# Random-feature attention with a mixture of experts: one burst of projections for each pair of the last batch, and its attention steps at fixed places

## The chip, the core and the metric

The kernel runs on one core of one Trainium2 chip. The metric is the device time of one execution in microseconds; the kernel before has a median of 872.78 us over three runs. The engines are named as the profile names them: PE (TensorE, with PEld for its weight loads), DVE (VectorE), ACT (ScalarE), POOL (GpSimd), and SP (SyncE), which here only issues DMA transfers.

## What is computed

Two layers, the second fed by the first. The attention has 4 batches, 8 heads, 576 positions, head size 64 and 128 random features:

```python
def phi(x):
    proj = np.einsum('bhsd,md->bhsm', x, omega)
    h = proj - np.sum(x * x, axis=-1, keepdims=True) / 2.0
    h = h - np.max(h, axis=-1, keepdims=True)
    return np.exp(h) / np.sqrt(m)
q_p, k_p = phi(q_s), phi(k_s)
kv = np.einsum('bhsm,bhsd->bhmd', k_p, v)
num = np.einsum('bhsm,bhmd->bhsd', q_p, kv)
den = np.einsum('bhsm,bhm->bhs', q_p, k_p.sum(axis=2))[..., None] + 1e-06
attn = num / den
```

The result, 2304 rows of 512, goes through 4 experts with F = 1024: `out += p[:, e] * (relu(x @ w1[e]) @ w2[e])`.

## The kernel before, in words

**Visits.** The expert part is cut into visits. A visit takes one half (512 of the 1024 hidden columns) of one expert's weights and one block of rows; products in fp32 are made of three matmuls on a high and a low part of each operand (`hh`/`hl`, `w2h`/`w2l` and so on). Four groups of visits follow each other: the first block of rows (functions `first_visit` and `plain`), then eight visits `N0` to `N0 + 7` on the second block of 768 rows (`fast`), then eight on the last rows (`deep`). The change touches the eight `fast` visits, which run from about 280 to 549 us of the trace. The rows of the last block are the output of the attention on the last batch, so the attention of that batch (four pairs of heads, class `Halves`) has to be worked in between the expert matmuls of the `fast` visits.

**A fast visit.** First come 14 small products (L967, 6 matmuls of 384 columns each), called p1 to p7 for each of two column groups. p1, p6, p7 and p4 of a group add onto the same PSUM bank `u`, so PE starts p6 only once ACT has copied p1 out of the bank into an SBUF tile `sum` (L973, `keep`), and p7 only once it has copied p6. Between them `split_w2` makes `w2h` on ACT (L642) and `w2l` on POOL out of freshly loaded `w2r`. Then come six output tiles of 12 matmuls of 512 columns (L830 to L832); of tiles 0, 1 and 2 the first six matmuls are made already among the products. Each finished tile is added to `acc` by DVE (`gather`, L842; in the first of the eight visits ACT does it, L840). Between the tiles the weights of the next visit are prepared (`sides`: four additions on DVE, L761 to L764, then `w1sh` on ACT, L642, and a subtraction on POOL).

**Attention of a pair.** Loads of k, q and v; `square` (POOL) and `lengths` (DVE, L340); projection of keys or queries onto the features (`project`, 16 matmuls, L351, and `project_tails`, 4 matmuls, L366, all on 64 rows of the array); maxima over features (DVE, L371 and L376) and `bias` (L381, L382, result `nbk` or `nbq`); exponentials (ACT, L388 in two halves of four, L395 for the tails, results `kp` and `qp`); `sum_keys` (PE, ACT, DVE), `turn` (transposes of the query features), `numerators`, `invert` (reciprocals, L303) and `times`.

**What sets the order.** The kernel is scheduled by hand: an instruction stands in its engine's queue where the Python code calls it, each engine works its queue in order, and waits on other engines are added. `fast` is a generator; each `yield` is a share, counted 0 (before tile 0's second half) to 6 (after tile 5). The loop at the end of `emit` takes one share after another and, whenever the count of shares is due, one tick of the attention generator (`opening` for the first pair's loads, then `later_ticks`, 12 ticks per pair). PSUM has eight banks that are handed out in rotation (`bank`, eight buffers of one tag). SP's loads carry eight semaphores in turn (`DMAHW0` to `DMAHW7` below): a load waits until the one eight places earlier in SP's queue has landed.

Of the kernel before, what the change touches and what calls it, by code (L numbers as in the profile page):

```python
# [5 lines left out]

F32 = mybir.dt.float32
F32R = mybir.dt.float32r
# [6 lines left out]
def attention_moe(ctx, tc, kT, qT, kd, qd, kn, qn, vn, omT, probs, w1, w2, out):  # L15
# [11 lines left out]
    _, NP, D, _ = kT.shape  # L27
# [3 lines left out]
    E, FP, P, _ = w1.shape  # L31
# [36 lines left out]
    def bank(name):  # L68
        return psum.tile([P, 512], F32, tag="ps", name=name)
# [33 lines left out]
    NV = len(HALVES)  # L103
# [339 lines left out]
    def opening(p, both=False):  # L443

        p.load("k")
        yield
        p.load("q")
        yield
        p.load_v()
        p.load_tails()  # L450
        yield
        p.square("k")
        yield
        p.square("q")
        yield
        p.lengths("k")
        if both:
            p.lengths("q")
        yield
# [71 lines left out]
        p.times(1)  # L531
        yield

    def later_ticks(pairs):

        for p, then in zip(pairs, pairs[1:] + [None]):
            p.project("k")
            p.project_tails("k")
            p.maxima("k")
            p.maxima_tails("k")  # L540
            p.bias("k")
            yield
            p.exp_tails("k")
            p.exp("k", 0)
            p.lengths("q")
            yield
            p.exp("k", 1)
            yield
            p.project("q")
            p.project_tails("q")  # L550
            p.maxima("q")
            p.maxima_tails("q")
            p.bias("q")
            yield
            p.exp_tails("q")
            p.exp("q", 0)
            if then:
                then.load("k")
            yield
            p.exp("q", 1)  # L560
            if then:
                then.load("q")
            yield
            p.sum_keys()
            if then:
                then.load_v()
                then.square("k")
            yield
            p.turn(0)
            yield  # L570
            p.turn(1)
            if then:
                then.square("q")
            yield
            p.numerators(0)
            if then:
                then.lengths("k")
            yield
            p.invert(0)
            p.times(0)  # L580
            p.numerators(1)
            yield
            p.invert(1)
            p.times(1)
            yield

    def visit(u, n, c0, m):
        return (u, *HALVES[n], c0, m)
# [1 line left out]
    BIG = {1: (START, 6 * P), 2: (START + 6 * P, 8 * P)}  # L590
# [5 lines left out]
    N0 = len(visits)  # L596
    visits += [visit(u, n, *BIG[u]) for u in (1, 2) for n in range(NV)]
    DEEP = range(N0 + NV, len(visits))
# [344 lines left out]
    def on_sides2(v):  # L943
        if v in sides2:
            next(sides2[v][1])

    def fast(v):
# [109 lines left out]
        for t in range(tiles):  # L1057
            if t in g2:
                outputs(v, hs, g2[t], t, range(2, FH))
            else:  # L1060
                g2[t] = bank("g2")
                outputs(v, hs, g2[t], t, range(FH))
            gather(v, g2[t], t)
            gathered(v, t)
            if t < 2:
                on_sides2(v + 1)
            next(ready, None)
            for _ in range(2 if t < 4 else 1):
                next(more, None)
            yield 1  # L1070
        for _ in more:
            pass

# [381 lines left out]
    def first_visit(g1):  # L1455
        hs = [relu(ps, 2 * P) for ps in g1[:2]]
        yield 0.5
        for ps in g1[2:]:
            split_w(lo=nc.vector)
            hs.append(relu(ps, 2 * P))  # L1460
            yield 0.5
        split_w(lo=nc.vector)
        split_w(lo=nc.vector)
        yield 0.5
        for t in range(2):
            ps = bank("g2")
            outputs(0, hs, ps, t, range(FH))
            gather(0, ps, t)
            gathered(0, t)
            split_w()  # L1470
            split_w(lo=nc.vector)
            yield 1
# [56 lines left out]
        pairs[3].settle()  # L1529
        yield  # L1530

    def chain(*many):
        for x in many:
            yield from x

    building = build(1)

    def emit():
        pairs, g1 = begin()
        later = [Halves(b, hp) for b in range(1, B) for hp in range(NP)]  # L1540
        windows = {
            0: (first_rest(pairs, opening(later[0], both=True)), 20 / 11),
            3: (joint_ticks(later[:-NP]), 76 / 45.4),
            N0: (chain(opening(later[-NP]), later_ticks(later[-NP:])), 54 / (NV * (BIG[1][1] // P + 1) * 0.8)),
        }
        ticks, n, done, per = iter(()), 0, 0.0, 0
        for v in range(len(visits)):
            if v in windows:
                for _ in ticks:
                    pass  # L1550
                ticks, per = windows[v]
                n, done = 0, 0.0
            for share in first_visit(g1) if v == 0 else deep(v) if v in DEEP else fast(v) if v >= N0 else plain(v):
                done += share
                while n < done * per:
                    next(ticks, None)
                    n += 1
        store(0)
# [62 lines left out]
```

## Time and profile before

| | |
|---|---|
| median of three runs | 872.78 us (871.76 to 873.16) |
| profiled execution | 872.62 us, span 870.8 us |
| PE busy | 865.4 us, 99% of the span |
| DVE, ACT, POOL busy | 578.8, 480.2, 559.6 us |
| DMA moved | 136.04 MB, mean 156 GB/s |
| granted TensorE clock | 1.000 |

The span is the time from the first to the last instruction in the profiled execution; its execution time lies 1.8 us above it. PE is busy nearly without a break, so a change of the time is either work that PE no longer has or a gap that opens or closes in its row. The other engines matter where PE has to wait for them.

### The profile page before, as it was taken

To read this page: it belongs to the slowest core of one execution; us is meant where nothing else is said; L and a number is where in the kernel's file an instruction comes from. 1 tells how busy PE (TensorE), PEld (TensorE's weight loads), DVE (VectorE), ACT (ScalarE), POOL (GpSimd) and SP (SyncE) were. 2 spreads that over 40 slices of the span, in tenths; PEclk is the share of its full clock that TensorE was granted. 3 is DMA by queue.
4 is the path that set the end of the run, shared out by engine and by line. 5 is a ranking of instruction groups with operands and counts; after the bars stand their busy time and mean duration, and the time that the engine had idled before them with its cause. 6 is when DMAs were issued, how large, how long until landed. Compare 5 with 4: busy or idle time off the path is not lost.

```text
span 870.8 us, 13397 instructions
## 1 busy us (share of the span) xinstructions
PE 865.4 (99%) x4791; PEld 752.9 (86%) x4791; DVE 578.8 (66%) x953; ACT 480.2 (55%) x1078; POOL 559.6 (64%) x523
## 2 busy tenths in 40 slices
PE   9999999999999999999999999999999999999998
PEld 9988898989888988989989899888888888888886
DVE  5666566666667547465756657885857577585757
ACT  6786677776774555556545554544534434453442
POOL 6759475655644554354444446769888797988865
PEclk9999999999999999999999999999999999999999
DMA  8765634524521756546274354835352462535222
GB/s 185 193 205 161 214 100 164 177 81 131 184 65 58 284 158 254 195 163 218 75 281 157 135 218 154 269 132 183 85 181 80 139 193 85 158 86 181 70 99 97
DMA packets 67651, 136.04 MB, mean 156 GB/s; under 512 B 10400, under 2 KB 23168, under 8 KB 67584
## 3 DMA queue, kind: packets, MB, share of 16 engines
q1 hardware_dynamic: 57488, 105.24, 36.7%
q0 software_dynamic: 9216, 29.36, 10.3%
q10 hardware_dynamic: 880, 0.57, 0.3%
q8 instruction: 38, 0.62, 0.3%
q14 instruction: 29, 0.24, 0.1%
HBM read 101.06 MB, written 34.10 MB: 155 GB/s over the span
## 4 chain that ended last, share of the span: by engine, by line
PE 95%; DMA 2%; POOL 1%; ACT 0%; SPq 0%; issue 0%; ACTq 0%; DVE 0%; POOLq 0%
PE g L1146 18%; PE g L1115 18%; PE g L967 14%; PE g L830 8%; PE g L831 8%; PE g L832 8%; PE g L815 3%; PE g L816 3%; PE g L817 3%; PE kv L406 2%; PE k_ps L351 2%; PE q_ps L351 1%; PE qt_ps L417 1%; DMA q<-in_qT 1%; PE nd L290 1%; PE nd L289 1%
## 5 line engine op out<-in xcount | busy, mean ns | idle before, releaser
L645 POOL TENSOR_TENSOR w2l<-w2r,w2h 128x512 fp32r<-128x512 f32 x61 | 79.3, 1311 | 76.4 <-ACT w2h L642 65.9
L645 POOL TENSOR_TENSOR w1sl<-w1r,w1sh 128x512 fp32r<-128x512 f32 (+1 forms) x43 | 75.2, 1751 | 59.0 <-ACT w1sh L642 52.7
L830 PE MATMUL g<-w2h,hh 128*128 128x512 f32 x280 | 111.6, 399 | 0.0
L832 PE MATMUL g<-w2h,hl 128*128 128x512 f32 x280 | 109.6, 391 | 0.0
L831 PE MATMUL g<-w2l,hh 128*128 128x512 f32 x280 | 109.5, 391 | 0.0
L645 POOL TENSOR_TENSOR w1al<-w1r,w1ah 128x512 fp32r<-128x512 f32 (+1 forms) x45 | 49.4, 1113 | 60.7 <-ACT w1ah L642 55.4
L1160 DVE TENSOR_TENSOR acc<-g,acc 128x512 f32<-128x512 f32 (+1 forms) x106 | 68.5, 681 | 27.2 <-PE g L1146 27.1
L842 DVE SCALAR_TENSOR_TENSOR acc<-g,pr,acc 128x512 f32<-128x512 f32 x70 | 51.0, 735 | 28.0 <-PE g L832 27.9
L832 PEld LDWEIGHTS g<-w2h,hl 128*128 128x128 f32 x280 | 52.5, 188 | 11.5
L830 PEld LDWEIGHTS g<-w2h,hh 128*128 128x128 f32 x280 | 52.6, 188 | 10.1
L831 PEld LDWEIGHTS g<-w2l,hh 128*128 128x128 f32 x280 | 52.6, 188 | 9.0
L1121 ACT ACTIVATE sum<-g 128x512 f32<-128x512 f32 x48 | 28.8, 600 | 48.1 <-PE g L1115 47.5
L981 ACT ACTIVATE hh<-sum 128x384 fp32r<-128x384 f32 x48 | 25.1, 525 | 50.8 <-DVE sum L979 50.4
L645 POOL TENSOR_TENSOR t_hl<-va,t_hl 128x1024 fp32r<-128x1024 f32 x16 | 38.8, 2426 | 21.2 <-ACT t_hl L642 21.2
L985 DVE SCALAR_TENSOR_TENSOR hl<-sum,hh 128x384 fp32r<-128x384 f32 x48 | 27.4, 575 | 36.9 <-ACT hh L981 36.2
L303 DVE RECIPROCAL dn<-dn 128x256 f32<-128x256 f32 (+1 forms) x24 | 46.5, 1943 | 6.3 <-ACT dn L297 6.2
L645 POOL TENSOR_TENSOR w2s<-w2f,w2s 128x512 fp32r<-128x512 f32 x30 | 38.5, 1308 | 18.1 <-ACT w2s L642 18.1
L1115 PE MATMUL g<-xbh,w1sh 128*128 128x512 f32 x128 | 49.9, 390 | 0.0
L1115 PE MATMUL g<-xbl,w1sh 128*128 128x512 f32 x128 | 49.8, 389 | 0.0
L1115 PE MATMUL g<-xbh,w1sl 128*128 128x512 f32 x128 | 49.8, 389 | 0.0
L979 DVE TENSOR_TENSOR sum<-g,sum 128x384 f32<-128x384 f32 x48 | 26.5, 555 | 33.3 <-PE g L967 27.6
L642 ACT ACTIVATE w1sh<-w1r 128x512 fp32r<-128x512 f32 (+1 forms) x43 | 34.1, 795 | 25.2 <-DVE w1r L764 12.9
(254 smaller groups left out, 2700.4 us busy)
## 6 DMA issues: line engine op xcount, KB each, us to landing
w1r<-in_w SPq DMA_DIRECT2D x54, 512.0 KB, 3.6
w2r<-in_w SPq DMA_DIRECT2D x76, 256.0 KB, 3.0
kept<-w1sh SPq DMA_DIRECT2D x16, 512.0 KB, 5.0
kept<-w1sl SPq DMA_DIRECT2D x16, 512.0 KB, 5.5
w1sh<-kept POOLq DMA_DIRECT2D x16, 512.0 KB, 4.6
w1sl<-kept POOLq DMA_DIRECT2D x16, 512.0 KB, 5.4
kept<-w1ah SPq DMA_DIRECT2D x16, 384.0 KB, 4.8
kept<-w1al SPq DMA_DIRECT2D x16, 384.0 KB, 4.9
```

The costliest lines, as they stand in the source:

```text
L303: nc.vector.reciprocal(dn, dn)
L642: hi.activation(a, t, AF.Copy)
L645: lo.tensor_tensor(c, t, f32(a), ALU.subtract)
L830: nc.tensor.matmul(ps, ha[:, ts_], wa, start=(c == 0), stop=False)
L831: nc.tensor.matmul(ps, ha[:, ts_], wc, start=False, stop=False)
L832: nc.tensor.matmul(ps, hc[:, ts_], wa, start=False, stop=(c == FH - 1))
L842: nc.vector.scalar_tensor_tensor(acc[i], ps, sc, acc[i], ALU.mult, ALU.add)
L967: nc.tensor.matmul(ps, a[:, w], x[:, k], start=(start and k + at == 0), stop=(k == 1 and at == 2), skip_group_check=not start)
L1115: nc.tensor.matmul(ps, a[:, w], x[:, k], start=(start and k + at == 0), stop=(k == 1 and at == 2), skip_group_check=not start)
L1121: nc.scalar.activation(t, P_[g][where], AF.Copy)
L1146: nc.tensor.matmul(ps[:, cs], y[:, w], x[:, cs], start=(start and f + k == 0), stop=(f + k == 3), skip_group_check=not start)
L1160: nc.vector.tensor_tensor(t[:, cs], ps[i][:, cs], t[:, cs], ALU.add)
```

## The change

The generator `later_ticks` (printed above) with its 12 ticks for each of the last four pairs is replaced by a table of steps, `later_steps`. A step is bound to a visit and a share; a pair has nine consecutive steps, which begin at places 2, 15, 24 and 36, counted in shares of the eight visits (seven in each): visit `N0` share 2, `N0 + 2` share 1, `N0 + 3` share 3 and `N0 + 5` share 1.

- Keys and queries of a pair are projected in one burst. The tails of the queries go into free columns of the two banks that hold the tails of the keys (`beside="k"`), so a burst takes six banks. The maxima of the queries are taken only after the exponentials of the keys' tails.
- The loads of the first pair (k, q, v: seven transfers) are issued near the end of visit `N0 - 1`; its squares and lengths come in the first two shares of `N0`. Before, they were ticks inside `N0`.
- The order of a pair's later steps is drawn together: `sum_keys` and the first `turn` stand in one step.
- In `fast`, `yield 1` moves ahead of the preparation of the next visit's weights, so that an attention step bound to a share now stands in front of that preparation on ACT, DVE and POOL.

The number of matmuls does not change.

```diff
-    def later_ticks(pairs):
...
+    def later_steps(pairs, at):
+
+        PER = BIG[1][1] // P + 1
+
+        steps = {}
+
+        def add(v, t, *calls):
+            steps.setdefault((N0 + v + t // PER, t % PER) if v >= 0 <= t else (N0 + v, t), []).extend(calls)
+
+        p = pairs[0]
+        add(-1, 13, partial(p.load, "k"), partial(p.load, "q"), p.load_v, p.load_tails)
+        add(0, 0, partial(p.square, "k"), partial(p.square, "q"))
+        add(0, 1, partial(p.lengths, "k"), partial(p.lengths, "q"))
+
+        for p, then, first in zip(pairs, pairs[1:] + [None], at):
+
+            def projections(p=p):
+                p.project("k")
+                p.project_tails("k")
+                p.project("q")
+                p.project_tails("q", beside="k")
+                largest(p, "k")
+
+            def largest(p, which):
+                p.maxima(which)
+                p.maxima_tails(which)
+                p.bias(which)
+
+            def keys(p=p):
+                p.exp("k", 0)
+                p.exp_tails("k")
+                largest(p, "q")
+
+            def queries(p=p):
+                p.exp("k", 1)
+                p.exp_tails("q")
+                p.exp("q", 0)
...
+            row = [
+                [projections],
+                [keys] + ([partial(then.load, "k")] if then else []),
+                [queries] + ([partial(then.load, "q")] if then else []),
+                [partial(p.exp, "q", 1)],
+                [sums_of],
+                [partial(p.turn, 1)] + ([partial(then.square, "k")] if then else []),
+                [partial(p.numerators, 0)] + ([partial(then.square, "q")] if then else []),
+                [rest] + ([partial(then.lengths, "k")] if then else []),
+                [last] + ([partial(then.lengths, "q")] if then else []),
+            ]
...
             if t < 2:
                 on_sides2(v + 1)
+            yield 1
             next(ready, None)
             for _ in range(2 if t < 4 else 1):
                 next(more, None)
-            yield 1
...
-            N0: (chain(opening(later[-NP]), later_ticks(later[-NP:])), 54 / (NV * (BIG[1][1] // P + 1) * 0.8)),
+            N0: (iter(()), 0),
         }
+        steps = later_steps(later[-NP:], (2, 15, 24, 36))
```

**Place 1: SP's queue in visit `N0`.** SP's queue before, from the load of the next visit's first weights (`w1r`) on; `out` are finished rows of the first block that are stored, `w2r` the second weights, `kept` copies that are written out for the last visits:

```order
L627 DMA w1r<-in_w 128x1024 [waits DMAHW0_49,Pool_49]
L856 DMA out<-acc 128x512 [waits DVE_49]
L856 DMA out<-acc 128x512 [waits DMAHW2_49,DVE_49]
L627 DMA w2r<-in_w 128x512 [waits DMAHW3_49,Pool_49]
L627 DMA w2r<-in_w 128x512 [waits DMAHW4_49,Pool_49]
L627 DMA w2r<-in_w 128x512 [waits DMAHW5_49,Pool_49]
L747 DMA kept<-w1ah 128x768 [waits DMAHW6_49]
```

The same place after the change:

```order
L643 DMA w1r<-in_w 128x1024 [waits DMAHW0_49,Pool_49]
L333 DMA k<-in_kd 128x576 [waits PE_49]
L333 DMA k<-in_kn 128x576 [waits DMAHW2_49]
L333 DMA q<-in_qd 128x576 [waits DMAHW3_49,PE_49]
L333 DMA q<-in_qn 128x576 [waits DMAHW4_49]
L140 DMA va<-in_vn 128x4x128 [waits DMAHW5_49,PE_49]
L144 DMA vb<-in_vn 64x4x64 [waits DMAHW6_49]
L145 DMA vb<-in_vn 64x4x64 [waits DMAHW7_49]
L872 DMA out<-acc 128x512 [waits DMAHW0_49,DVE_49]
L872 DMA out<-acc 128x512 [waits DMAHW1_49,DVE_49]
L643 DMA w2r<-in_w 128x512 [waits DMAHW2_49,Pool_49]
```

Seven loads of the first pair now stand between `w1r` and the two stores, and the first `w2r` waits for the landing of the second of them (`k<-in_kn`, which carries `DMAHW2`).

**Place 2: DVE and PE at the second pair's burst, visit `N0 + 2`.** DVE's queue before, where `acc<-g` is the gather of an output tile, `t_ps<-k_ps` and the four rows behind it are the maxima and the bias of the keys, and `sqq` the lengths:

```order
L303 RECIPROCAL dn<-dn 128x320
L371 TENSOR_REDUCE t_ps<-k_ps 128x4 [waits PE_49]
L371 TENSOR_REDUCE t_ps<-k_ps 128x4 [waits DVE_49]
L376 TENSOR_REDUCE t_ps<-t_ps 64x1 [waits DVE_49]
L376 TENSOR_REDUCE t_ps<-t_ps 64x1 [waits DVE_49,PE_49]
L381 SCALAR_TENSOR_TENSOR t_ps<-sqk,t_ps 128x9 [waits DVE_49]
L382 SCALAR_TENSOR_TENSOR nbk<-sqk,t_ps 128x9 [waits DVE_49]
L842 SCALAR_TENSOR_TENSOR acc<-g_4524,pr,acc 128x512 [waits PE_49]
L340 TENSOR_REDUCE sqq<-q 128x9 [waits Pool_49]
L842 SCALAR_TENSOR_TENSOR acc<-g_4540,pr,acc 128x512 [waits PE_49]
```

After, from the gather of tile 0 on:

```order
L858 SCALAR_TENSOR_TENSOR acc<-g_4526,pr,acc 128x512 [waits PE_49]
L372 TENSOR_REDUCE t_ps<-k_ps 128x4 [waits PE_49]
L372 TENSOR_REDUCE t_ps<-k_ps 128x4 [waits DVE_49]
L377 TENSOR_REDUCE t_ps<-t_ps 64x1 [waits DVE_49]
L377 TENSOR_REDUCE t_ps<-t_ps 64x1 [waits DVE_49,PE_49]
L382 SCALAR_TENSOR_TENSOR t_ps<-sqk,t_ps 128x9 [waits DVE_49]
L383 SCALAR_TENSOR_TENSOR nbk<-sqk,t_ps 128x9 [waits DVE_49]
L858 SCALAR_TENSOR_TENSOR acc<-g_4542,pr,acc 128x512 [waits PE_49]
L372 TENSOR_REDUCE t_ps<-q_ps 128x4 [waits Activation_49]
```

PE's queue after, the last six matmuls of tile 2 and the first of tile 3:

```order
L846 MATMUL g_4572<-w2h,hh 128x512
L847 MATMUL g_4572<-w2l,hh 128x512
L848 MATMUL g_4572<-w2h,hl 128x512
L846 MATMUL g_4572<-w2h,hh 128x512
L847 MATMUL g_4572<-w2l,hh 128x512
L848 MATMUL g_4572<-w2h,hl 128x512
L846 MATMUL g_4683<-w2h,hh 128x512 [waits DVE_49]
```

The maxima of the keys moved from ahead of tile 0's gather to between tile 0's and tile 1's, and tile 3's first matmul (`g_4683`) waits for DVE's release of a bank, that is for the gather of tile 1 just ahead of the queries' maxima; before, the first matmul of tile 3 waits for ACT.

**Place 3: DVE and ACT at the third pair's burst, end of visit `N0 + 3`.** DVE's queue before, from the first reciprocal of the second pair to the gather of tile 3 (the gather of tile 2 is the second row):

```order
L303 RECIPROCAL dn<-dn 128x256 [waits Activation_49]
L842 SCALAR_TENSOR_TENSOR acc<-g_4961,pr,acc 128x512 [waits PE_49]
L303 RECIPROCAL dn<-dn 128x320 [waits Activation_49]
L371 TENSOR_REDUCE t_ps<-k_ps 128x4 [waits PE_49]
L371 TENSOR_REDUCE t_ps<-k_ps 128x4 [waits DVE_49]
L376 TENSOR_REDUCE t_ps<-t_ps 64x1 [waits DVE_49]
L376 TENSOR_REDUCE t_ps<-t_ps 64x1 [waits DVE_49,PE_49]
L381 SCALAR_TENSOR_TENSOR t_ps<-sqk,t_ps 128x9 [waits DVE_49]
L382 SCALAR_TENSOR_TENSOR nbk<-sqk,t_ps 128x9 [waits DVE_49]
L842 SCALAR_TENSOR_TENSOR acc<-g_5074,pr,acc 128x512 [waits PE_49]
```

After, from the gather of tile 0 to the first maximum of the keys:

```order
L858 SCALAR_TENSOR_TENSOR acc<-g_4924,pr,acc 128x512 [waits PE_49]
L304 RECIPROCAL dn<-dn 128x256 [waits Activation_49]
L341 TENSOR_REDUCE sqk<-k 128x9 [waits Pool_49]
L858 SCALAR_TENSOR_TENSOR acc<-g_4940,pr,acc 128x512 [waits PE_49]
L304 RECIPROCAL dn<-dn 128x320 [waits Activation_49]
L341 TENSOR_REDUCE sqq<-q 128x9 [waits Pool_49]
L777 TENSOR_TENSOR w1r<-w1r 128x256 [waits DMAHW4_49]
L778 TENSOR_TENSOR w1r<-w1r 128x256 [waits DVE_49]
L779 TENSOR_TENSOR w1r<-w1r 128x256 [waits DVE_49]
L780 TENSOR_TENSOR w1r<-w1r 128x256 [waits DVE_49]
L858 SCALAR_TENSOR_TENSOR acc<-g_4970,pr,acc 128x512 [waits PE_49]
L372 TENSOR_REDUCE t_ps<-k_ps 128x4 [waits PE_49]
```

ACT's queue before, from the preparation `w1sh` to the first `keep` of visit `N0 + 4` (`sum<-g`) and the `w2h` behind it:

```order
L642 ACTIVATE w1sh<-w1r 128x1024
L395 ACTIVATE kp<-t_ps,nbk 64x128 x2
L388 ACTIVATE kp<-k_ps,nbk 128x128 x4
L642 ACTIVATE w1sh<-w1r 128x1024
L388 ACTIVATE kp<-k_ps,nbk 128x128 x4
L973 ACTIVATE sum<-g_5170 128x384
L642 ACTIVATE w2h<-w2r 128x512
```

After:

```order
L658 ACTIVATE w1sh<-w1r 128x1024
L389 ACTIVATE kp<-k_ps,nbk 128x128 x4
L396 ACTIVATE kp<-t_ps,nbk 64x128 x2
L389 ACTIVATE kp<-k_ps,nbk 128x128 x4
L396 ACTIVATE qp<-t_ps,nbq 64x128 x2
L389 ACTIVATE qp<-q_ps,nbq 128x128 x4
L658 ACTIVATE w1sh<-w1r 128x1024
L389 ACTIVATE qp<-q_ps,nbq 128x128 x4
L989 ACTIVATE sum<-g_5183 128x384
L658 ACTIVATE w2h<-w2r 128x512
```

On DVE both reciprocals, two lengths and four additions now stand ahead of tile 2's gather and of the keys' maxima. On ACT the exponentials of the queries (`qp`) stand ahead of the first `keep` of the next visit; before, they came behind it.

## Rows read from the trace of the kernel before

**Rows 1.** Windows: stretch, us, each engine's busy time (instructions), clock, DMA share, GB/s.

```profile
280.00:549.00 269.00, 268.51 (x1513) 242.28 (x1512) 166.89 (x292) 145.50 (x325) 127.28 (x100) 1.00 0.54 193
```

**Rows 2.** Timeline of PE at one key burst and one query burst (start, us, instruction, idle).

```profile
305.99 1.16 PE L351 MATMUL k_ps<-om_r,k 64*128 64x128 f32 x16 [0.49 <-DMA k<-in_kd]
...
331.17 0.39 PE L831 MATMUL g<-w2l,hh 128*128 128x512 f32 x1
331.40 0.40 PE L832 MATMUL g<-w2h,hl 128*128 128x512 f32 x1
331.73 1.16 PE L351 MATMUL q_ps<-om_r,q 64*128 64x128 f32 x16
...
333.04 0.50 PE L830 MATMUL g<-w2h,hh 128*128 128x512 f32 x1
333.38 0.39 PE L831 MATMUL g<-w2l,hh 128*128 128x512 f32 x1
```

**Rows 3.** Chain of waits in order of time: start, us, what; one visit's product phase.

```profile
313.04 11.46 PE g L967 x66
```

**Rows 4.** Timeline of the SP queue, 283 to 302 us.

```profile
284.20 0.34 SPq L627 DMA_DIRECT2D w1r<-in_w  x1
284.59 1.42 SPq L856 DMA_DIRECT2D out<-acc  x2
286.17 5.48 SPq L627 DMA_DIRECT2D w2r<-in_w  x3
```

**Rows 5.** Windows: a stretch in which the DMA engines are fully busy.

```profile
300.00:304.00 4.00, 4.00 (x20) 3.30 (x19) 1.70 (x4) 3.35 (x6) 2.05 (x3) 1.00 1.01 353
```

**Rows 6.** DMA issues: count, size of one, median us to landing.

```profile
w2r<-in_w SPq DMA_DIRECT2D x76, 256.0 KB, 3.0
```

**Rows 7.** Timeline of ACT at the end of the first fast visit's products.

```profile
291.25 0.62 ACT L642 ACTIVATE w2h<-w2r 128x512 fp32r<-128x512 f32 x1
291.77 0.48 ACT L973 ACTIVATE sum<-g 128x384 f32<-128x384 f32 x1
```

**Rows 8.** Timeline of PE there.

```profile
292.60 0.34 PE L967 MATMUL g<-xbh,w1sh 128*128 128x384 f32 x1
```

**Rows 9.** Timeline of DVE at a joint burst of the first block.

```profile
81.27 1.43 DVE L371 TENSOR_REDUCE t_ps<-k_ps 128x4 f32<-128x512 f32 x2 [3.03 <-PE t_ps L366]
...
83.68 0.17 DVE L382 SCALAR_TENSOR_TENSOR nbk<-sqk,t_ps 128x9 f32<-128x9 f32 x1
```

**Rows 10.** Timeline of DVE in the fourth fast visit.

```profile
408.08 0.75 DVE L842 SCALAR_TENSOR_TENSOR acc<-g,pr,acc 128x512 f32<-128x512 f32 x1
...
412.55 1.74 DVE L303 RECIPROCAL dn<-dn 128x256 f32<-128x256 f32 x1
...
414.78 2.14 DVE L303 RECIPROCAL dn<-dn 128x320 f32<-128x320 f32 x1
416.84 1.37 DVE L371 TENSOR_REDUCE t_ps<-k_ps 128x4 f32<-128x512 f32 x2
...
419.93 0.41 DVE L761 TENSOR_TENSOR w1r<-w1r 128x256 f32<-128x256 f32 x1
...
421.64 0.75 DVE L340 TENSOR_REDUCE sqq<-q 128x9 f32<-128x576 f32 x1
```

**Rows 11.** Timeline of PE there: the first and the last of six matmuls.

```profile
409.96 0.30 PE L288 MATMUL nd<-qth,kvh 128*128 128x320 f32 x1
...
410.70 0.31 PE L290 MATMUL nd<-qtl,kvh 128*128 128x320 f32 x1
```

**Rows 12.** Timeline of ACT there.

```profile
419.44 0.75 ACT L395 ACTIVATE kp<-t_ps,nbk 64x128 f32<-64x128 f32 x2 [5.68 <-PE g L832]
420.22 1.14 ACT L388 ACTIVATE kp<-k_ps,nbk 128x128 f32<-128x128 f32 x4
421.80 1.06 ACT L642 ACTIVATE w1sh<-w1r 128x1024 fp32r<-128x1024 f32 x1 [0.44 <-issue]
...
424.71 0.49 ACT L973 ACTIVATE sum<-g 128x384 f32<-128x384 f32 x1 [0.81 <-PE g L967]
```

More of the change, by code (lines that the diff above doesn't have):

```diff
@@ L5 @@
 from concourse.masks import make_identity
+from functools import partial
 F32 = mybir.dt.float32
@@ L532, in divided @@
         yield
-    def later_ticks(pairs):
[L536 to L585, printed above, removed]
@@ new lines, in later_steps, with sums_of, rest, last @@
+    def later_steps(pairs, at):
[26 more added lines that the diff above has]
+                p.exp("q", 0)
+            def sums_of(p=p, then=then):
+                p.sum_keys()
+                if then:
+                    then.load_v()
+                p.turn(0)
+            def rest(p=p):
+                p.invert(0)
+                p.times(0)
+                p.numerators(1)
+            def last(p=p):
+                p.invert(1)
+                p.times(1)
+            row = [
[9 more added lines that the diff above has]
+            ]
+            for i, calls in enumerate(row):
+                add(0, first + i, *calls)
+        return steps
@@ L1530, in first_rest @@
         yield
-    def chain(*many):
-        for x in many:
-            yield from x
     building = build(1)
@@ L1552, in emit @@
                 n, done = 0, 0.0
-            for share in first_visit(g1) if v == 0 else deep(v) if v in DEEP else fast(v) if v >= N0 else plain(v):
+            for step in steps.get((v, -1), ()):
+                step()
+            for i, share in enumerate(first_visit(g1) if v == 0 else deep(v) if v in DEEP else fast(v) if v >= N0 else plain(v)):
+                for step in steps.get((v, i), ()):
+                    step()
                 done += share
```

## The prediction

> **What bounds the kernel now.** I read the windows first. In the stretch of the eight fast visits, 280 to 549 us, PE is busy 268.51 of 269.00 us at full clock, while DVE, ACT and POOL have 102 us and more to spare [rows 1]. So nothing there can get faster except by what PE itself does, and any new wait of PE goes straight into the time; the deep visits behind depend on PE in the same way and can't give it back. Two things can therefore be gained: the 0.49 us that PE stands idle, and time inside PE's row that is no matmul work. The timeline of PE shows both. The 0.49 us are one wait for the first load of keys [rows 2]. At a projection burst the row loses time at either edge: matmuls of 512 columns start every 0.23 us (331.17 to 331.40), but the first projection comes 0.33 us after the last of them (331.40 to 331.73), and the second matmul behind the burst 0.34 us after the first (333.04 to 333.38). That is 0.10 and 0.11 us for the change to matmuls on 64 rows and back [rows 2].
>
> **What the change saves.** Four pairs, each with one burst instead of two: 4 x 0.21 = 0.84 us. The first keys are now issued right behind `w1r` (284.20) [rows 4] and land near 290, by the working of wait 1 below; their burst, behind tile 1, has still 18 small and 24 large matmuls ahead of it when PE starts p7 at 292.60 [rows 8], 8.6 us, and comes near 301. So the wait of 0.49 us goes. Together 1.3 us, and no other PE time is removed, since the matmuls are the same. This is an upper bound of the gain: 0.15% of the time, less than the 0.2% (1.75 us) by which this kernel's measurements can tell a change. A clear gain is therefore nearly excluded; the question is which waits come.
>
> **New wait 1: SP's queue in `N0`.** Before, SP issues `w1r` at 284.20, two stores, and the three `w2r` from 286.17 [rows 4]. After, seven loads stand between. The first `w2r` is what ACT's `w2h` at 291.25 reads, and behind that on ACT stands the `keep` of p6 (291.77 to 292.25) [rows 7]; PE starts p7, which adds onto that bank, at 292.60 [rows 8]. So the slack is 0.35 us. Price from above: if the transfers run one after the other, then from 284.20 there are `w1r` 512 KB, keys and queries 4 x 288 KB, values 256 + 2 x 64 KB, stores 2 x 256 KB and `w2r` 256 KB, 2816 KB or 2.88 MB. At 353 GB/s, the rate of a stretch in which the DMA engines are full [rows 5], that is 8.2 us; a `w2r` of 256 KB, 0.74 us at this rate, lands 3.0 us after its issue [rows 6], so 2.3 us come on top: 294.7. `w2h` and `keep` (0.62 + 0.48) end at 295.7, and PE waits 295.7 - 292.6 = 3.1 us. From below: `w2r` is issued when `k<-in_kn` has landed, after 512 + 576 KB or 3.2 us + 2.3 us, at 289.7, and lands by itself 3.0 us later at 292.7; `keep` ends at 293.7 and PE waits 1.1 us. I take 2.5, nearer to the upper end, because the row of a full stretch shows the engines saturated with fewer transfers in flight than SP has here. The Trainium skill ("DMA: Bandwidth & Descriptors", Queues, rings and completion order) says that each DMA engine consumes its ring's descriptors in the order of issue; by that the wait would be the 3.1 us of the upper end, and no run here has shown it yet.
>
> **New wait 2: tile 3 behind the second and the fourth pair's burst.** Both bursts stand after tile 0. A burst takes six of eight banks and tiles 1 and 2 hold the others, so tile 3 can start only when the gather of tile 1 has freed one. In DVE's queue the keys' maxima and bias stand ahead of that gather. At a joint burst of the first block they begin when the burst's last matmul has run and end 2.58 us later (81.27 to 83.85) [rows 9]; the gather takes 0.75 [rows 10]. So 3.33 us after the burst the bank is free, while PE has 12 matmuls of 0.2275 us, 2.73 us, left. PE waits 0.6 us, twice: 1.2 us. Below, 0.4 each if DVE's work overlaps as its rows of before do by some 0.08 us; above, 1.2 each if ACT's exponentials, which stand ahead of the first `turn`, come late too (by my sum they have 0.2 to 0.3 us left). The Trainium skill ("Perfetto Trace Analysis", Identifying Performance Opportunities) says that the same gap repeating on the engine that should be saturated can mean there isn't enough PSUM for the next tile. Applied here it speaks against joint bursts, by the same 0.6 us a time; the trace of before shows no such repeated gap, its whole idle time being one of 0.49 us.
> The first pair's burst stands after tile 1, and 18 matmuls (4.1 us) lie between it and the first tile that needs its bank; 3.33 us fit into that, so it costs nothing.
>
> **New wait 3: the third pair's burst, end of visit `N0 + 3`.** Count from the end of tile 0. PE: 6 matmuls of tile 1 (1.37), six matmuls of the second pair's numerators, one each 0.15 us, 0.9 [rows 11], tile 2 (1.37), the burst (2 x 1.31), tile 3 (2.73): tile 4 starts at 9.0, tile 5 at 11.7. DVE: gather 0.75, reciprocal 1.74, lengths 0.75, gather 0.75, reciprocal 2.14, lengths 0.75, four additions 1.71 (419.93 to 421.64), gather of tile 2 0.75 [rows 10], 9.3 us less about 0.5 for the overlap of neighbours (a reciprocal of 2.14 is followed after 2.06): 8.8. Tile 4 just gets its bank. Then the keys' maxima, 2.58: 11.4, and the gather of tile 3: 12.1, for which tile 5 waits 0.35 us. PE ends tile 5 at 14.85, and p1, p2 and p5 of the next visit, 18 matmuls of 0.174 us (11.46/66) [rows 3], take it to 18.0, where p6 must have p1's `keep`. ACT meanwhile: at 11.4 the first exponentials and the tails of the keys, 1.14 + 0.75 [rows 12], 13.3; then DVE's maxima and bias of the queries, as long as those of the keys, 2.58, 15.8; then on ACT the queries' tails 0.75, four exponentials 1.14, `w1sh` 1.06, four exponentials 1.14, and only then `keep`, 0.49 [rows 12]: 4.58 less 0.35 of overlaps, 20.0. PE waits 2.05 us for it. In the kernel before, `keep` ran at 424.71, just behind p1 [rows 12], since the queries' exponentials came later. Together 2.4 us; below 1.6, if the first DVE sum is shorter by a length that runs earlier; above 3.5, if the additions wait for their load.
>
> **The sum.** Waits 2.5 + 1.2 + 2.4 = 6.1, savings 1.3, net 4.8 us. The profiled execution took 872.62 us, 0.16 below the median of the runs shown: 872.62 + 4.8 = 877.4, which I give as **877.5**. What is left out at no price: first lengths and squares in `N0`, on POOL and DVE, which have 102 us and more to spare [rows 1] and which nothing waits for before the burst; if that cover were gone, a length costs 0.75 us [rows 10] on a queue, not on PE. `sum_keys` and `turn` in one step stand in PE's row at the same length as before. The moved `yield` puts attention steps ahead of the additions, whose result `w1sh` has a whole tile and more to arrive.
>
> **The rivals.**
> (a) *The queue of SP doesn't hold `w2r` up*, since transfers share the engines or `w2r` isn't late: wait 1 falls to at most 0.3 us. Time 877.4 - 2.4 = 875.0. For it: the kernel before has three transfers and more in flight without a break of PE. Against: the order in SP's queue and the semaphores. 2 in 10.
> (b) *The third pair's `keep` isn't late*, because DVE reaches the keys' maxima earlier: 877.4 - 2.1 = 875.3. Under 1 in 10.
> (c) *Not slower: the copy of p1 and p6 doesn't decide when PE may go on.* Waits 1 and 3 both act at one place, the bank `u` that ACT must have copied. In the trace of before PE never stood idle for that copy; all its idle time is the 0.49 us [rows 1, 2]. If PE's wait there is met earlier than I read it, 2.5 + 2.05 us go and 872.62 + 1.2 + 0.35 - 1.3 = 872.9 is left, no change. It decides when the two together cost under 1.5 us. 13 in 100.
> (d) *The other way round, more waits:* each late exponential of the second and fourth pair holds `turn`, 0.6 each, and the loads in `N0` also delay the stores and copies behind them: up to 882. 1 in 10.
> (e) *Only the savings:* 871.3, still within 0.2%. 3 in 100.
>
> **How the numbers follow.** All three waits as summed: about 5 in 10, by itself 876 to 879.5. With (a), (b) and part of (d) the range 874.3 to 881.0 holds 8 in 10; (c) and (e) lie below it. Slower by over 0.2% (above 874.5) are the forecast, (a), (b) and (d): 0.82; within 0.2% (c) and (e): 0.15; faster: 0.03.
>
> **What the profile of the changed kernel would show.** No idle time of PE ahead of the first burst of `N0`, and eight edges of 0.10 us instead of sixteen. A gap of about 2.5 us in PE ahead of p7 near 292, with `w2h` on ACT waiting for its load until about 294. Two gaps of 0.6 us ahead of tile 3, put down to a gather of DVE, in `N0 + 2` and `N0 + 5`. A gap of about 2 us between p5 and p6 of `N0 + 4`, put down to ACT's `sum`, with `qp` rows just ahead of it. PE's busy time less by under 1 us, its idle time in the stretch near 6 us. The prediction is wrong if these gaps don't show, above all the two at the bank `u`, or if PE waits inside a burst for one of its six banks, which I count at nothing because the last of them is the one that tile 0's gather frees while the first half of the burst runs.

## The result: 1% slower, just above the range

The changed kernel takes 881.24 us (median of five runs, 880.02 to 881.66) against 872.72 before; the ratio is 1.0099, 95% interval 1.0088 to 1.0109. The forecast was 877.5 us, with 881.0 as its upper end. The direction and the three places of the forecast came out. But one of the three waits cost more than the upper end given for it, and two costs were not in the sum at all.

The profiled execution has a span of 879.3 us, 8.5 more than before. Windows, same columns as [rows 1], show that the deep visits behind take no longer and that the stretch of the fast visits holds the loss. In the kernel before, the fast visits end at 560.9 us, where the first deep matmul starts, and not at 549; what [rows 1] leaves out has no idle time of PE. The fast visits and then the deep ones, before:

```profile
279.70:560.80 281.10, 280.61 (x1566) 252.30 (x1566) 178.42 (x303) 153.49 (x334) 135.88 (x110) 1.00 0.56 197
560.80:870.80 310.00, 306.41 (x1352) 252.43 (x1350) 215.35 (x328) 130.29 (x220) 253.48 (x242) 1.00 0.40 126
```

The same two stretches in the changed kernel:

```profile
280.20:569.30 289.10, 282.10 (x1567) 253.45 (x1566) 187.10 (x303) 153.34 (x334) 136.31 (x110) 0.99 0.55 192
569.30:879.30 310.00, 306.36 (x1352) 252.38 (x1350) 215.24 (x328) 130.34 (x220) 253.77 (x242) 1.00 0.40 126
```

In the fast visits PE is idle 7.0 us, not 0.49, and its mean clock is 0.99. The view of waits of PE in that stretch (engine and line, what is waited for: total, times, longest) names what it waits for:

```profile
PE g L983 <- ACT sum L989: 6.0, 3, 3.1
PE g L846 <- DVE acc L858: 0.8, 2, 0.4
```

Three waits for ACT's copy `sum`, two for DVE's gather. The timeline of PE has the places (time in brackets is idle time, then the releaser):

```profile
292.92 0.39 PE L848 MATMUL g<-w2h,hl 128*128 128x512 f32 x1
296.41 0.44 PE L983 MATMUL g<-xbh,w1sh 128*128 128x384 f32 x1 [3.10 <-ACT sum L989]
...
357.82 0.34 PE L983 MATMUL g<-xbh,w1sl 128*128 128x384 f32 x1
359.22 0.44 PE L983 MATMUL g<-xbh,w1sh 128*128 128x384 f32 x1 [1.06 <-ACT sum L989]
...
382.24 0.50 PE L846 MATMUL g<-w2h,hh 128*128 128x512 f32 x1 [0.38 <-DVE acc L858]
...
432.85 0.34 PE L983 MATMUL g<-xbh,w1sl 128*128 128x384 f32 x1
435.07 0.45 PE L983 MATMUL g<-xbh,w1sh 128*128 128x384 f32 x1 [1.88 <-ACT sum L989]
```

In order: ahead of p7 of `N0`; ahead of p6 of `N0 + 2`; ahead of tile 3 of `N0 + 2`, with its twin of the same length in `N0 + 5`; ahead of p6 of `N0 + 4`. Counted from the start of the matmul ahead of a gap to the start of the one behind it, less what a matmul takes (0.23 or 0.17 us), they cost 3.26, 1.23, 0.54 twice and 2.05 us; a small one of 0.29 ahead of tile 5 of `N0 + 3` belongs to the last. Together that is 7.9 us. Below, "by spacing" means this count. The second was not in the forecast. Nor was this: windows of 1 us behind the first gap (same columns; the figure before the DMA share is the granted clock):

```profile
297.00:298.00 1.00, 1.00 (x7) 0.95 (x6) 0.24 (x1) 0.00 (x0) 0.39 (x1) 0.96 1.03 416
298.00:299.00 1.00, 1.00 (x4) 0.71 (x3) 0.41 (x2) 0.52 (x1) 0.00 (x0) 0.50 1.04 425
299.00:300.00 1.00, 1.00 (x4) 0.81 (x3) 0.47 (x1) 0.00 (x0) 0.00 (x0) 0.50 1.02 418
300.00:301.00 1.00, 1.00 (x5) 1.00 (x4) 0.00 (x0) 0.00 (x0) 0.00 (x0) 0.50 1.01 408
301.00:302.00 1.00, 1.00 (x6) 1.00 (x6) 0.24 (x1) 0.00 (x0) 0.00 (x0) 0.83 1.08 433
```

For about 3.4 us (all of three slices and parts of the two at the ends) the clock stands at its lower level of 1.2 GHz (0.50), and ten matmuls that take 2.0 us at full clock take 3.6 (297.79 to 301.38 in the timeline): 1.6 us more. The books close: 7.9 + 1.6, less about 1.4 for the wait for keys and the saved edges, is 8.1; the fast visits take 8.0 us longer by the windows, and the first block ended 0.5 us later in this execution.

**Wait 1 as it is.** SP's queue and ACT in the changed kernel, answering to [rows 4] and [rows 7]:

```profile
284.74 0.34 SPq L643 DMA_DIRECT2D w1r<-in_w  x1
285.13 0.42 SPq L333 DMA_DIRECT2D k<-in_kd  x1
285.61 0.42 SPq L333 DMA_DIRECT2D k<-in_kn  x1
...
289.90 2.57 SPq L643 DMA_DIRECT2D w2r<-in_w  x3
```

```profile
295.35 0.63 ACT L658 ACTIVATE w2h<-w2r 128x512 fp32r<-128x512 f32 x1 [3.45 <-DMA w2r<-in_w]
295.88 0.47 ACT L989 ACTIVATE sum<-g 128x384 f32<-128x384 f32 x1
```

The three `w2r` are issued at 289.90 and later instead of 286.17, the first lands near 295.3, and p7 starts at 296.41.

**Wait 3 as it is.** ACT ahead of p6 of `N0 + 4`, answering to [rows 12]:

```profile
432.52 1.08 ACT L658 ACTIVATE w1sh<-w1r 128x1024 fp32r<-128x1024 f32 x1
433.47 1.16 ACT L389 ACTIVATE qp<-q_ps,nbq 128x128 f32<-128x128 f32 x4
434.47 0.54 ACT L989 ACTIVATE sum<-g 128x384 f32<-128x384 f32 x1
```

The copy of p1 comes right behind the queries' exponentials, as forecast.

**The gap that was not forecast.** DVE, POOL and ACT ahead of p6 of `N0 + 2`:

```profile
350.35 2.14 DVE L304 RECIPROCAL dn<-dn 128x320 f32<-128x320 f32 x1
...
353.67 2.47 DVE L777 TENSOR_TENSOR w1r<-w1r 128x256 f32<-128x256 f32 x1
356.17 0.42 DVE L778 TENSOR_TENSOR w1r<-w1r 128x256 f32<-128x256 f32 x1
356.63 0.42 DVE L779 TENSOR_TENSOR w1r<-w1r 128x256 f32<-128x256 f32 x1
```

```profile
352.63 0.88 POOL L442 TENSOR_TENSOR raw_x<-nu,dn 128x320 f32<-128x320 f32 x1 [4.06 <-DVE dn L304]
353.47 2.39 POOL L661 TENSOR_TENSOR w1sl<-w1r,w1sh 128x1024 fp32r<-128x1024 f32 x1
```

```profile
357.60 1.06 ACT L658 ACTIVATE w1sh<-w1r 128x1024 fp32r<-128x1024 f32 x1 [6.69 <-DVE w1r L780]
358.68 0.49 ACT L989 ACTIVATE sum<-g 128x384 f32<-128x384 f32 x1
```

The first addition takes 2.47 us where its neighbours take 0.42. It begins 0.2 us after POOL's subtraction for `w1sl` and ends 0.3 us after it. `w1sh`, which needs the additions, starts at 357.60, the copy of p1 stands behind it on ACT, and PE stands still until 359.22. POOL's subtraction is that late because the product with the reciprocal (352.63) stands ahead of it: POOL waited 4.06 us for DVE's reciprocal.

### The profile page after: what moved, and what is told of

The parts are those of the page before. It is cut to its first block, busy times and chain, and to the rows that moved or that the text cites. A ratio compares the mean times of both kernels' runs of the same rounds, so it can differ in the third digit from the quotient of the medians.

```text
span 879.3 us, 13392 instructions
## 1 busy us (share of the span) xinstructions
PE 865.9 (98%) x4791; PEld 752.8 (86%) x4791; DVE 587.4 (67%) x953; ACT 480.2 (55%) x1078; POOL 560.3 (64%) x523
## 4 chain that ended last, share of the span: by engine, by line
PE 86%; DVE 9%; DMA 2%; issue 1%; ACT 1%; SPq 0%; POOL 0%; DVEq 0%; ACTq 0%; POOLq 0%
PE g L1162 17%; PE g L1131 16%; PE g L983 12%; PE g L846 7%; PE g L847 7%; PE g L848 7%; PE g L831 3%; PE g L832 3%; PE g L833 3%; PE kv L407 2%; DVE xbl L661 2%; DVE acc L858 1%; PE k_ps L352 1%; PE qt_ps L418 1%; PE q_ps L352 1%
## 5 line engine op out<-in xcount | busy, mean ns | idle before, releaser
L1001 DVE SCALAR_TENSOR_TENSOR hl<-sum,hh 128x384 fp32r<-128x384 f32 x48 | 30.0, 632 | 36.9 <-ACT hh L997 36.3
L983 PE MATMUL g<-xbh,w1sh 128*128 128x384 f32 x128 | 43.6, 340 | 6.0 <-ACT sum L989 6.0
```

The lines of the kernel that those rows point to most:

```text
L983: nc.tensor.matmul(ps, a[:, w], x[:, k], start=(start and k + at == 0), stop=(k == 1 and at == 2), skip_group_check=not start)
L1001: nc.vector.scalar_tensor_tensor(x, y, 0.0, f32(z), ALU.max, ALU.subtract)
```

## The experiments

Times are medians; ratios to the kernel before on the same chip with their 95% interval. Gaps without another word are idle times of PE by the profile.

**1. First pair's loads two shares earlier** (`e1_loads_earlier`).

```diff
-        add(-1, 13, partial(p.load, "k"), ...
+        add(-1, 11, partial(p.load, "k"), ...
```

> The changed kernel with one number altered: the first pair's seven loads are issued two shares earlier in the visit ahead of N0, so that SP has them in front of the w1r that waits until about 284.7 us, and out of the way of the w2r behind it. Theory (SP's queue): the w2r is issued near 286 again, ACT's w2h and the copy of p6 come in time, PE's gap of 3.10 us ahead of p7 goes, and with it the stretch of about 3 us at half clock behind the gap, which costs some 1.6 us: 881.2 - 3.3 - 1.6 = 876.3. The gaps of 0.54, 1.06, 0.54 and 2.05 us stay. Rival 1 (half clock has nothing to do with the gap): the gap goes and the slow stretch stays somewhere, 877.9. Rival 2 (w2r is late for the volume of transfers and not for its place): nothing moves, 881.

877.1 us, ratio 1.0045 (1.0032 to 1.0057). SP issues `w2r` at 285.95 again and the gap ahead of p7 is gone.

```profile
285.95 5.48 SPq L643 DMA_DIRECT2D w2r<-in_w  x3
```

But a stretch at half clock is now behind the gap at p6 of `N0 + 4`:

```profile
429.40:432.90 3.50, 3.48 (x12) 3.49 (x13) 0.55 (x1) 1.87 (x4) 3.46 (x3) 0.56 0.39 94
```

So it can stand behind another gap than that ahead of p7. Two of the five executions had a mean clock of 1.000 and took 875.1 and 875.6 us, three had 0.997 or 0.998 and took 877.1 to 877.6. By these times the stretch costs about 2 us where it comes. Place in SP's queue: shown, and rival 2 falls. Rival 1 does not fall here: the gap went, a slow stretch stayed elsewhere, as it says, and 877.1 lies between the 876.3 of the theory and its 877.9. That each slow stretch stands behind a gap speaks against it; experiment 8 decides.

**2. Third pair one share earlier** (`e2_third_pair_after_tile1`): places `(2, 15, 23, 36)`.

> The changed kernel with one number altered: the third pair begins one share earlier, so that its burst stands after tile 1 of N0 + 3 instead of after tile 2, as the first pair's does. Theory (ACT's queue at the bank u): the queries' exponentials are done before the visit ends, PE's gap of 2.05 us ahead of p6 of N0 + 4 goes and the 0.29 us ahead of its tile 5 as well: 881.2 - 2.3 = 878.9; a new wait of up to 0.3 us at a tile is possible, since a reciprocal and a length of the second pair now stand ahead of the keys' maxima. Rival (the exponentials are late because DVE is held up throughout, so the gap only moves one tile): 880.5 to 881.5, with a gap of 1 us or more still ahead of p6.

880.46 us, 1.0084 (1.0071 to 1.0098). The gap at p6 of `N0 + 4` is gone, as the theory of ACT's queue says, but a gap of 1.10 us opens at tile 4, where ACT's `kp` is late because DVE's reciprocal and length now stand ahead of the keys' maxima, and one of the kind of `N0 + 2` at p6 of `N0 + 5`, again with an addition of 2.47 us. The gap moved more than it went: the rival was right about the gaps. The median alone would not tell: two of the five executions, with a mean clock of 1.000, took 878.87 and 879.45 us, near the theory's 878.9, and three with 0.996 to 0.998 took 880.46 to 881.75.

**3. The yield back** (`e3_yield_back`).

```diff
-            yield 1
             next(ready, None)
...
+            yield 1
```

> The changed kernel with the moved yield put back behind the preparation of the next visit's weights; the table of steps stays. Theory (queue of POOL and DVE): the gap of 1.06 us ahead of p6 of N0 + 2 comes from the attention standing ahead of the preparation: POOL's product with the reciprocal stands ahead of the subtraction for w1sl, which then runs at 353.5 to 355.9, while DVE's first addition takes 2.47 us instead of 0.42, and w1sh and the copy of p1 behind it on ACT are late. With the yield back that gap goes: 881.2 - 1.2 = 880.0. Other gaps (3.10, 0.54 twice, 2.05) within 0.5 us of what they are. Rival (the reciprocals of the first pair are late by their place in the table, with either order): no gap less, 881.2 within 0.5.

878.84 us, 1.0070 (1.0058 to 1.0083). The gap at p6 of `N0 + 2` is gone, the additions there take 0.41 to 0.43 us, and the rival falls:

```profile
354.12 0.41 DVE L777 TENSOR_TENSOR w1r<-w1r 128x256 f32<-128x256 f32 x1
354.56 0.43 DVE L778 TENSOR_TENSOR w1r<-w1r 128x256 f32<-128x256 f32 x1
```

The gap at p6 of `N0 + 4` falls from 1.88 to 1.1, and one of 0.45 opens at the first pair's first `turn`. 2.4 us were gained, more than the 1.2 expected.

**4. Loads alone, in the kernel before** (`e4_before_loads_at_13`): the seven loads as in the changed kernel, all ticks as before.

> The kernel before with one part of the change alone: the first pair's loads are issued where the changed kernel issues them, at the end of the visit ahead of N0; all later ticks stay as before. Theory (SP's queue): the first w2r of N0 lands near 294 to 295, PE waits about 3.3 us ahead of p7, the clock falls to its lower level for about 3 us behind it (1.6 us more), and the 0.49 us wait for the keys goes: 872.7 + 3.3 + 1.6 - 0.5 = 877.1. Rival (the loads alone do no harm, and the gap needs the squares and lengths or the moved yield): 872.2.

879.09 us, 1.0073 (1.0061 to 1.0086): this one part, which takes a wait of 0.49 us away, costs 6.5 us.

```profile
295.84 0.69 PE L970 MATMUL g<-xbh,w1sh 128*128 128x384 f32 x1 [3.41 <-ACT sum L976]
```

PE is idle 3.41 us ahead of p7. The slow stretch behind it lasts to 301.8 and costs 2.9 us by spacing: 17 matmuls, which take 3.27 us at full clock, take 6.14 (295.84 to 301.98). A gap of 1.1 us by spacing follows at p6 of `N0 + 1`. The rival falls. The time lies 2.0 us above the 877.1 expected, which had 1.6 us for the slow stretch and nothing for the last gap.

**5. The same loads two shares earlier, in the kernel before** (`e5_before_loads_at_11`).

> The kernel before with the first pair's loads issued two shares earlier than the changed kernel does, ahead of the w1r that waits; all else as before. Theory (place in SP's queue decides): no gap ahead of p7 of N0, the 0.49 us wait for the keys goes, and the half-clock stretch doesn't come: 872.6 - 0.5 = 872.1, against 879.1 for the same loads two shares later. The 1.10 us gap ahead of N0 + 1's p6 that the later loads left goes too. Rival (seven loads that early harm at any place, since they share the DMA engines with the weights): 875 or more.

873.78 us, 1.0017 (1.0009 to 1.0026). 5.3 us better than experiment 4: the place decides. But it is not the gain that was expected. A gap of 1.2 us is left at p6 of `N0 + 1`, and DVE and POOL show why:

```profile
303.91 1.35 DVE L764 TENSOR_TENSOR w1r<-w1r 128x256 f32<-128x256 f32 x1 [1.89 <-POOL w1al L648]
305.30 2.48 DVE L765 TENSOR_TENSOR w1r<-w1r 128x256 f32<-128x256 f32 x1
307.81 1.25 DVE L766 TENSOR_TENSOR w1r<-w1r 128x256 f32<-128x256 f32 x1
309.10 0.42 DVE L767 TENSOR_TENSOR w1r<-w1r 128x256 f32<-128x256 f32 x1
```

```profile
303.84 1.14 POOL L336 TENSOR_TENSOR k<-k 128x576 f32<-128x576 f32 x1
304.95 2.54 POOL L648 TENSOR_TENSOR w1sl<-w1r,w1sh 128x1024 fp32r<-128x1024 f32 x1
307.45 1.33 POOL L336 TENSOR_TENSOR q<-q 128x576 f32<-128x576 f32 x1
```

With the keys there early, POOL's squares run right ahead of the subtraction, and three of DVE's additions take 1.35, 2.48 and 1.25 us beside them. Before, POOL idled 2.41 us waiting for a load, and the additions fell into that.

**6. Yield back and loads earlier** (`e9_loads_earlier_yield_back`), **7. the same with all bursts after tile 1** (`e7_after_tile1_yield_back`, places `(2, 16, 23, 37)`).

> The changed kernel with two repairs: loads two shares earlier and the yield back; places 2, 15, 24, 36 stay. By adding up the two single repairs: gaps of about 0.76 (first turn), 0.54, 0.29, 1.28 and 0.54 us stay, 3.4 together, savings 1.3: 872.6 + 2.1 = 874.7; taken from the run with the yield back alone less its gap of 3.39 and its slow stretch of 1.54, 873.9. Theory on the clock (PE's clock falls behind a gap of 2 us or more): none is left, so no stretch at half clock. Rival (the clock falls once in this part of the program, whatever the gaps): a slow stretch of about 1.5 us shows up behind a shorter gap, 875.5.

874.62 us, 1.0024 (1.0015 to 1.0033), clock 1.000: as added up. The longest gap is 1.1 us and no slow stretch is left. The theory's length of 2 us is not borne out: in experiment 1 the stretch followed a gap of 1.88 us.

> The changed kernel with three repairs: loads two shares earlier, the yield back, and all four bursts after tile 1 (places 2, 16, 23, 37). Theory (the gaps of 0.54 us come from the keys' maxima ahead of tile 1's gather, and after tile 1 there are 4.1 us of PE work for 3.3 us of DVE): both gaps of 0.54 go; the third pair still meets the second pair's reciprocals and keeps a gap of about 1.3 us at tile 4; about 0.8 us stay at the first pair's first turn: 872.6 - 1.3 + 2.1 = 873.4. Rival (the place after tile 0 is not what costs): gaps of 0.5 stay, 874.5.

874.09 us, 1.0023 (1.0014 to 1.0033), between the theory's 873.4 and the rival's 874.5. The profile decides: both gaps of 0.54 are gone, so the place after tile 0 is what costs them; the third pair has one of 1.4 us at tile 4, and the first `turn` of the first and of the third pair wait 1.1 us together.

**8. PE kept busy while it waits** (`e10_filled`, on top of experiment 3; the 18 matmuls' result is not used).

```diff
         begun(0)
+        if v == N0:
+            fill = bank("fill")[:, :n]
+            (wa, _), (xa, _) = W[v, "w1", 1][7], X[7]
+            for _ in range(18):
+                nc.tensor.matmul(fill, wa[:, :P], xa[:, 0], start=True, stop=True)
         p7(1)
```

> The changed kernel with the yield back, and 18 matmuls of 384 columns (3.1 us), whose result nobody reads, set into PE's queue of N0 ahead of p7, where PE otherwise stands idle for 3.2 us: PE is busy while it waits for ACT's copy. Theory (the clock falls because PE stood idle): the wait takes as long as before, but no stretch at half clock follows: 878.8 - 1.5 = 877.3, mean clock 1.000. Rival (the clock falls for the load of DMA or the like at this place): slow stretch as before, 878.8 or a little more.

878.51 us, 1.0073 (1.0061 to 1.0086). The profile of visit `N0`, first without and then with the filling matmuls:

```profile
279.30:321.45 42.15, 38.48 (x219) 34.20 (x218) 23.88 (x42) 22.54 (x51) 17.84 (x13) 0.96 0.63 226
```

```profile
280.35:321.45 41.10, 40.05 (x237) 35.92 (x236) 23.91 (x42) 22.57 (x51) 17.86 (x13) 1.00 0.64 232
```

The clock stays at 1.00, in all five executions (mean 0.999 to 1.000, against 0.997 to 0.999 without), and the visit is 1.05 us shorter though p7 starts 0.49 us later by spacing. So the clock falls because PE stood idle, and the rival falls. The median fell by only 0.3 us, not by the 1.5 expected. In this profile, the slowest of the five executions, the first block ended 1.05 us later, and the deep visits take 0.88 us longer, nearly all of it at one wait of PE for a load:

```profile
609.66 0.50 PE L1136 MATMUL g<-xbh,w1sl 128*128 128x512 f32 x1 [0.50 <-DMA w1sl<-kept]
```

What makes that load late, and whether the other four executions have the wait, was not tried: that the filling saves time is not shown.

**9. The product one share later** (`e8_times_later`): DVE's queue unchanged, POOL's `w1sl` ahead of the product.

```diff
                 p.invert(1)
-                p.times(1)
...
+                [partial(p.times, 1)],
```

> The changed kernel with one call moved: the second product with the reciprocal (POOL) becomes a step of its own one share later, so that it stands behind the subtraction for w1sl in POOL's queue and not ahead of it. DVE's queue stays word for word as it was. Theory (POOL and DVE hold each other up when both work on two operands in SBUF): w1sl runs near 351 instead of 353.5, DVE's first addition there takes 0.42 us and not 2.47, w1sh and the copy of p1 are in time, and the gap of 1.06 us ahead of p6 of N0 + 2 goes: 881.2 - 1.2 = 880.0. Rival (DVE's reciprocal and length ahead of the additions make w1sh late): the gap stays at 1 us, 881.2.

The gap at p6 of `N0 + 2` is gone: `w1sl` starts at 352.25 and the first addition takes 0.83 us.

```profile
351.61 2.14 DVE L304 RECIPROCAL dn<-dn 128x320 f32<-128x320 f32 x1
353.67 0.69 DVE L341 TENSOR_REDUCE sqq<-q 128x9 f32<-128x576 f32 x1
...
354.93 0.83 DVE L777 TENSOR_TENSOR w1r<-w1r 128x256 f32<-128x256 f32 x1
```

The reciprocal and the length stand ahead of the additions as before, so they were not the cause; the meeting of DVE and POOL was. The time did not follow: 881.94 us, 1.0107 (1.0093 to 1.0120). In the profiled execution, the slowest of four, the gap ahead of p7 was 3.9 us long, and two slow stretches came, behind that gap and behind the one at p6 of `N0 + 4`.

**10. Squares early as well, in the kernel before** (`e11_before_loads_and_squares_early`).

> The kernel before with the first pair's loads ahead of the waiting w1r, as in the run that gave 873.8, and its two squares on POOL in the first two ticks of N0 instead of the fourth and fifth. Theory (the 1.4 us gap of that run ahead of p6 of N0 + 1 comes from three additions that took 1.35, 2.48 and 1.25 us instead of 0.43 beside POOL's squares and subtraction): the additions fall into POOL's idle time again, the gap goes, and only the saving of the wait for the keys is left: 872.3 - 0.5 = 871.8. Rival (the earlier burst itself makes the gap, since ACT does the gathers in that visit): 873.8 again, with additions of 0.43 us.

873.52 us, 1.0011 (1.0002 to 1.0020). Half right: the gap fell from 1.2 to 0.8 us, but the additions are slow at other places now (0.85 to 1.40 beside the squares and the subtraction for `w1al`, 2.60 beside `w1sl`). The expected gain of 0.5 us over the kernel before did not come.

**11. Tails first** (`e12_tails_first`) and **12. tails first, second and fourth pair after tile 1** (`e13_tails_first_after_tile1`), both with loads earlier and the yield back.

```diff
-                p.exp("k", 0)
                 p.exp_tails("k")
+                p.exp("k", 0)
                 largest(p, "q")
```

> The run with loads two shares earlier and the yield back (874.6), with two calls swapped in each pair: ACT takes the exponentials of the keys' tails ahead of those of the first half, so that DVE can begin the maxima of the queries 1.14 us sooner. Theory (what holds PE at p6 of N0 + 4 and at the first pair's first turn is the chain keys' exponentials, tails, queries' maxima, queries' exponentials): the gap of 1.28 falls to 0.2 and that of 0.78 goes; 0.54, 0.29 and 0.54 stay: 874.6 - 1.9 = 872.7. Rival (ACT's own work, not the chain over DVE, is the limit there): gaps unchanged, 874.6.

873.29 us, 1.0010 (1.0001 to 1.0018). The gap at the first `turn` is gone; that at p6 of `N0 + 4` is not (1.2 us), since with the yield back four additions stand ahead of the queries' maxima there. Right for one of two places.

> The same as the run with the tails first, and the second and fourth pair one share later, after tile 1 (places 2, 16, 24, 37). Theory (tile 3 waits for a gather behind the keys' maxima only when the burst stands after tile 0): the two gaps of 0.54 go as well, and the kernel has the savings of the joint bursts nearly unspoilt: 872.7 - 1.1 = 871.6, 0.7 us below the kernel before. Rival (the second pair's later reciprocals now fall between the third pair's burst and its maxima, so the third pair pays): 873 or more, with a gap of 1 us or more at tile 4 or p6.

873.85 us, 1.0014 (1.0005 to 1.0023). The second and fourth pair cost at most 0.2 us, the third pays 1.9 us at tile 4, and a slow stretch follows. The rival was right. No version tried beats the kernel before.

## Why the prediction missed, step by step

- **What bounds the kernel, and the upper bound of the gain: right.** No kernel with joint bursts or early loads came below the kernel before, and the saved edges and the saved wait are in the books at 1.4 us, forecast 1.3.
- **Wait 1: right mechanism, wrong size.** "I take 2.5, nearer to the upper end": it cost 3.26 us by spacing, just above the upper end of 3.1 itself, and 3.1 to 3.9 idle in the kernels that keep this queue. Experiments 1, 4 and 5 show that the place in SP's queue does it. They don't separate the order in the queue from the load on the DMA engines, since two shares earlier these engines also had less to do (their share in the kernel before is 0.35 in 280 to 282 us and 0.00 in 282 to 284). The landings, issue plus the time to landing, speak for the order: the keys land at 289.0 and 289.8, the queries at 291.2 and 292.1, the values at 293.0 to 293.4, and the first `w2r` at 295.3, 5.4 us after its issue. That is the upper end's sum, 294.7, with a `w1r` issued 0.54 us later than before; the step that failed here is the choice of 2.5, below a sum that the transfers then followed. The Trainium skill ("DMA: Bandwidth & Descriptors", Queues, rings and completion order) says that each DMA engine consumes the descriptors of a ring in their order, and this trace agrees.
- **What a long gap does to the clock: missing from the sum.** The prediction's "any new wait of PE goes straight into the time" priced a wait at its length. The stretch at 1.2 GHz behind it came on top: 1.6 us in this profile, about 2 us in experiment 1, 2.9 in experiment 4. Experiment 8 shows the idle time as its cause. Nothing in the trace of before showed it, its clock being 1.000 and its longest gap 0.49 us.
- **Wait 2: right, 0.54 twice against 0.6;** experiment 7 shows the place after tile 0 as the cause. Within a burst PE waited for no bank, as forecast.
- **Wait 3: right, 2.05 + 0.29 against 2.05 + 0.35.** The copy ended at 435.01, 20.2 us after tile 0's end against 20.0 forecast. Experiment 2 adds that no place of that pair was free: the same DVE work delays something else one tile on.
- **The step that failed outright: the moved yield at no price.** "The moved `yield` puts attention steps ahead of the additions, whose result `w1sh` has a whole tile and more to arrive": that counted DVE's and ACT's queues, each with durations as of before, and left out that an addition of 0.42 us takes up to 2.5 while POOL works. It cost 1.23 us. Experiments 3 and 9 show it. The measured time is 0.24 us above the range: without any one of the three, the yield, the clock or the excess of wait 1, it would have been inside.
- **Rivals.** (a) fell with experiment 4. (b) and (e) fell. (c), that the copies don't decide, fell: 6.0 of 6.8 us of PE's waits are put down to them. (d) was right that more would come, but for other reasons. The chances as listed don't add up: the forecast, (a), (b) and (d) come to about 0.9, not 0.82, and (c) and (e) to 0.16, not 0.15; nothing hangs on it.

With 3.26 for 2.5, 1.23 for the yield and 1.6 for the clock, the forecast of 877.5 would have been 881.1.

## What to carry to other kernels

A load that is issued "early" is early only if nothing needed sooner stands behind it in the same queue: look for what waits anyway (here `w1r`, for some 5 us) and put the loads ahead of that. Where one engine is full, price a reordering by the queues of all engines and by which two of them then work at the same time, not by durations of the trace before. And a long gap of PE costs more than its length.

## What was not expected of the hardware

- **DVE and POOL hold each other up.** An addition of two SBUF tiles (128x256) on DVE takes 0.41 to 0.43 us alone and 2.47 to 2.60 beside POOL's subtraction of 2.4 us; it ends 0.3 us after that one ends. POOL loses less: in experiment 5 its subtraction takes 2.54 us and its second square 1.33, where the trace of before has 2.39 and 1.15. The Trainium skill ("SBUF — State Buffer", SBUF: two separate sides) says that a DVE instruction with two SBUF inputs and a GpSimd instruction that reads SBUF contend for a shared port pair, and that the one which starts first holds it for the whole instruction. The trace agrees: 353.47 to 355.86 on POOL, 353.67 to 356.14 on DVE.
- **PE's clock falls to 1.2 GHz behind gaps,** for 3.4 us in five profiled stretches, and for 6.8 us in three (experiments 2, 4 and 9), which began while PE still stood idle. In the profiles it did so behind each of the five idle gaps of 3.1 us and more, behind three of four of 1.8 to 1.9 us, and behind none of 1.4 us or less; with unread matmuls in place of the gap it did not. Whether it comes differs between executions of one kernel, as experiments 1 and 2 show. The Trainium skill ("TensorE: Matmul & The Clock Gate", Part 1) ties the clock to how busy PE has been lately, and the filled gap agrees.
